# Rwkv6 with a SiLU block: w handled a unit ahead, the state's decay on ScalarE, and another order of the diagonal

## The chip, the core and the metric

The kernel runs on one core of a Trainium2 chip. The core has five engines that run their own instruction streams and wait for each other through semaphores: TensorE (PE in the profile, its weight loads PEld), VectorE (DVE), ScalarE (ACT), GpSimd (POOL) and SyncE (SP), which here only issues transfers. The metric is the device time of one execution in microseconds, smaller is better. The kernel before takes 576.55 us, the median of 3 runs (576.12, 576.55 and 578.34).

## The reference

Two blocks follow each other. The first is a recurrence over 768 tokens, for 4 batches and 8 heads of 48 channels; the second is two matrix products with a SiLU between them, over the 3072 rows that the first one gives.

```python
for t in range(S):                                   # S = 768
    cur = einsum('bhd,bhe->bhde', u * k[t], v[t])
    y[t] = einsum('bhd,bhde->bhe', r[t], state + cur)
    state = w[t][..., None] * state + einsum('bhd,bhe->bhde', k[t], v[t])
x = y.transpose(0, 2, 1, 3).reshape(3072, 384)
h = x @ w_in                                         # 384 x 2048
out = (h * (1 / (1 + exp(-h)))) @ w_out              # 2048 x 384
```

## The kernel before, in words

**Units.** The work is cut into 12 units: 6 chunks of 128 tokens times 2 pairs of batches (`units`, L66). Unit 0 is the first, so the sixth is unit 5. A chunk is not run token by token. With products of w over 2, 4, 8 ... 128 tokens (`product`, L404: levels 0 to 6, each one POOL multiplication that halves the length), queries and keys are scaled level by level (`grow_queries` L621 on VectorE, `grow_keys` L639 and `grow_own` L648 on POOL, `odd_keys` L609 on ScalarE, `prepare` L776 and L778), multiplied on TensorE (`burst`, L697) and kept under a mask in `score` (`keep_level`, L715 on VectorE, L797 on ScalarE). `score` times v, and the state times the queries, give y (`y_state`, L840 and L847; `y_values`, L861). At the end of a chunk the state is multiplied by the product of the whole chunk's w (the decay, L911) and the products of k and v are added (L906 on TensorE, L920 on VectorE): `update`.

**The diagonal.** From unit 4 on the blocks of 8 x 8 tokens on the diagonal of `score` are made apart: `block_bonus` (L490 on POOL, steps 0 to 7) multiplies r, k, u and w elementwise in another layout (`tokens_rk`, `tokens_w`, loaded by `load_rk`, L158); `block_sum` (L527 on VectorE, steps 0 to 4) reduces them into `block_sums`; `block_move` stores these to memory (`kept`, one transfer, L549) and loads them back in the layout of `score` (five transfers, L554 and L556); `block_turn` (L560) and two `block_write` (L566) put them in. Sum 2 needs bonus step 4; sum 3 needs step 6; sum 4 needs step 7.

**Loads and turns.** w, k and r of a unit come in 4 blocks of 32 tokens for each (`load_blocks`, L127, 4 transfers a block, all issued on SP), into one room for each name. `turn` (L361, two VectorE transposes) puts them in the layout of the products; only then may the room be loaded again. v comes by `load_values` (L140 and L147, 5 transfers).

**The second block** is done with fewer multiplications by a Strassen-like scheme. For unit i-1 its first layer is 20 products (`ups`; `first_part`, L1141, 16 matmuls each, 0.87 us of TensorE). They run in the order 20, 18, 14, 13, 2, 15, 4, 7, 19, 16, 1, 12, 9, 11, 3, 6, 10, 5, 8, 17, in four PSUM banks that are reused. Between them are sums and differences of the banks (`join`, L1168 on VectorE), copies (L1162) and SiLUs (L1165, L1184) on ScalarE. So product 4 has to wait for the join behind 13, and product 17 for the join behind 10. The inputs of these products are made by `sums_of_x` (steps 0 to 7, VectorE, L1102 to L1122). The second layer of unit i-2 is 7 quarters (`downs`; `quarter`, L1284, 16 matmuls each, 2.6 us). Their inputs are made by `sums` (8 VectorE instructions, L1255); quarters 0, 2, 3 and 6 end with a copy on ScalarE (L1289), 1, 4 and 5 with a join on VectorE (L1292). Quarters 0, 2, 4 and 6 add into the same bank one after the other, so quarter 6 starts only when the join of quarter 4 has read it.

**The order** is written by hand. `mix(i)` gives 21 groups of steps for unit i, and the last loop puts between the groups the 27 steps `downs(i - 2) + ups(i - 1)`. Every engine gets its instructions in that order and waits in it. TensorE's order around a unit is: 7 quarters, the first `burst` behind quarter 6, products 20 to 11, the second burst, products 3 to 17, then the transposes of k and `y_state`, which end the unit. Group 0 stands ahead of quarters 0 and 1, group 1 ahead of quarter 2, group 2 of 3, group 3 of 4, group 4 of 5 and 6, group 5 of products 20 and 18, group 6 of 14, group 7 of 13, group 8 of 2 and 15, group 9 of 4, groups 10 to 13 of 7, 19, 16 and 1, group 14 of 12 and 9, group 15 of 11, group 16 of 3 and 6, group 17 of 10, group 18 of 5, group 19 of 8 and 17, and group 20 of the next unit's quarter 0.

Of the kernel before, what the change touches and what calls it, by code (L numbers as in the profile page):

```python
# [38 lines left out]
def kernel(  # L39
# [16 lines left out]
    NL = 7  # L56
# [841 lines left out]
    def update(i, b):  # L898
# [50 lines left out]
    def mix(i):  # L949
# [12 lines left out]
        def turns(j):  # L962
            return [*both(turn, j, "w"), (product, j, 0), *both(turn, j, "k")]

        def start(j):
            return [*[(product, j, l) for l in range(1, NL)], (grow_own, j, 1)]
# [16 lines left out]
        else:  # L983
            j = i - 1
            groups = [([*both(turn, i, "r"), (grow_own, i, 0), (x_out, j)], 2),
                      ([*start(i), *bonus_steps(i, 4), (x_in, j), (reverse_v, i)], 1),
                      ([(grow_queries, i, 2), (sums_of_x, j, 0)], 1),
                      ([(odd_keys, i, 2), (grow_keys, i, 2, False), (sums_of_x, j, 1)], 1),
                      ([(sums_of_x, j, 2), *sum_steps(i, 2), (prepare, i, 3), *bonus_steps(i, 5, 6, 7), (sums_of_x, j, 3, 4, 5, 6)], 2),
                      ([(burst, i, 3), (keep_level, i, 3)], 2),  # L990
                      ([*sum_steps(i, 3)], 1),
                      ([], 1),
                      ([*sum_steps(i, 4), (keep_level, i, 4)], 2),
                      ([(go_on, i, 4)], 1),
                      ([], 1),
                      ([*at(ahead, (load_rk, i + 1, (0, 1), nc.scalar)), (block_move, i, False), (block_move, i, True), *at(ahead, (load_rk, i + 1, (2,)))], 1),
                      ([], 1),
                      ([(sums_of_x, j, 7)], 1),
                      ([(prepare, i, 5)], 2),
                      ([], 1),  # L1000
                      ([(burst, i, 5), (keep_level, i, 5, 0), (keep_level, i, 6, 0), (go_on, i, 6), (block_turn, i), (block_write, i, 1)], 2),
                      ([(keep_level, i, 5, 1), (keep_level, i, 6, 1)], 1),
                      ([(block_write, i, 0)], 1),
# [439 lines left out]
```

## Time and profile before

| | |
|---|---|
| median of 3 runs | 576.55 us |
| profiled execution, whole | 580.51 us |
| its span, first to last instruction | 578.6 us |
| granted TensorE clock, mean | 0.997 |
| PE / DVE / POOL / ACT busy | 97% / 82% / 67% / 45% |
| from `y_state` to `y_state`, units 5 to 11 | 45.0, 44.1, 43.6, 43.3, 42.9, 44.6, 42.5 us |
| moved by transfers | 57.59 MB, 206485 packets |

In the rows, the first number of a timeline line is its start in us from the span's start, the second its length, and the brackets hold the idle time of the engine ahead of it and what ended it. A line of the waits has the total in us, how often, and the longest. Rows of the stretches show for each engine the busy time and the number of instructions, then the granted clock, the DMA engines' share and the GB/s. Instructions of an engine can overlap a little at their ends, so a pitch is taken from start to start.

### The profile page before, as it was taken

How to read it: one execution, taken by the hardware profiler on the slowest of the kernel's cores; microseconds unless marked ns; L12 is line 12 of the kernel's file. 1: busy time of each engine (PE TensorE's matmuls, PEld its weight loads, DVE VectorE, ACT ScalarE, POOL GpSimd, SP SyncE). 2: the span in 40 equal slices, each digit the busy share in tenths (PEclk: the TensorE clock that was granted, in tenths of full speed). 3: DMA queues.
4: the chain of work that ended last, by engine and by line, in shares of the span. 5: the costliest groups of instructions: out<-in, count | busy, mean ns of one | idle time of the engine just before them, and what ended most of it. 6: DMA issues, size and time to landing. Idle time of an engine off the chain costs nothing. (4 is left out here: it accounts for less than half of the span.)

```text
span 578.6 us, 18815 instructions
## 1 busy us (share of the span) xinstructions
PE 559.7 (97%) x7782; PEld 519.2 (90%) x7782; DVE 475.8 (82%) x748; ACT 259.1 (45%) x556; POOL 390.4 (67%) x459
## 2 busy tenths in 40 slices
PE   8989999999999899999999999999999989999997
PEld 8767777698899899999989989999999989999997
DVE  7979798898899999889889889889899878782250
ACT  5679695432541370371371372372371362371330
POOL 5998868547799997866866866866976966810000
PEclk9999999999999999999999999999999999999999
DMA  9957776444345453554554454464464452002000
GB/s 224 310 114 207 174 237 101 48 81 114 89 83 76 110 84 70 94 109 86 93 108 92 89 110 85 91 109 89 88 113 89 89 109 60 33 9 56 28 7 22
DMA packets 206485, 57.59 MB, mean 100 GB/s; under 512 B 186048, under 2 KB 198208, under 8 KB 206400
## 3 DMA queue, kind: packets, MB, share of 16 engines
q1 hardware_dynamic: 196272, 44.01, 39.0%
q10 hardware_dynamic: 10128, 12.39, 8.4%
q8 instruction: 61, 1.00, 0.8%
q14 instruction: 24, 0.20, 0.1%
HBM read 47.14 MB, written 9.18 MB: 97 GB/s over the span
## 5 line engine op out<-in xcount | busy, mean ns | idle before, releaser
L639 POOL TENSOR_TENSOR tk<-tk,tw 128x256 f32<-128x256 f32 x128 | 95.3, 765 | 37.0 <-ACT tk L609 27.3
L1284 PE MATMUL p_o<-own,temps 128*128 128x192 f32 x528 | 88.1, 326 | 0.2 <-DVE temps L1255 0.2
L1284 PEld LDWEIGHTS p_o<-own,temps 128*128 128x128 f32 x528 | 86.0, 190 | 0.6 <-DVE temps L1255 0.5
L1141 PE MATMUL p_o<-xt,w_in_sb 128*64 128x128 f32 x1152 | 73.4, 273 | 5.7 <-DVE p_o L1168 5.0
L407 POOL TENSOR_TENSOR tw<-tw 128x256 f32<-128x256 f32 (+6 forms) x83 | 42.4, 510 | 45.1 <-DVE tw L361 41.2
L1141 PEld LDWEIGHTS p_o<-xt,w_in_sb 128*64 128x64 f32 x1152 | 64.6, 137 | 7.1 <-DVE p_o L1168 6.2
L1034 PE MATMUL p_h<-xt,w_in_sb 128*128 128x256 f32 x288 | 66.1, 384 | 1.7 <-POOL w_in_sb L260 1.6
L1034 PEld LDWEIGHTS p_h<-xt,w_in_sb 128*128 128x128 f32 x288 | 53.6, 190 | 10.0 <-POOL w_in_sb L260 2.4
L1284 PE MATMUL p_o<-w_out_sb,gt 128*128 128x192 f32 x340 | 60.0, 329 | 1.6 <-DVE ob L1292 0.9
L490 POOL TENSOR_TENSOR ruk<-tokens_rk 128x384 f32<-128x384 f32 x48 | 54.1, 1148 | 11.1 <-DMA tokens_rk<-in_k_dram 6.8
L1284 PEld LDWEIGHTS p_o<-w_out_sb,gt 128*128 128x128 f32 x340 | 55.3, 190 | 2.8 <-DVE ob L1292 1.2
L1289 ACT COPY partial<-p_o 128x192 f32<-128x192 f32 x33 | 10.5, 319 | 92.3 <-PE p_o L1284 77.5
L621 DVE TENSOR_TENSOR tr<-tr,tw 128x512 f32<-128x512 f32 x61 | 51.3, 841 | 0.5
L609 ACT COPY tk<-tk 128x256 f32<-128x256 f32 x52 | 20.9, 402 | 64.6 <-POOL tk L639 44.6
L1255 DVE TENSOR_TENSOR temps<-gt 128x512 f32<-128x512 f32 (+1 forms) x48 | 43.3, 940 | 0.0
L1165 ACT ACTIVATE gt<-p_o 128x512 f32<-128x512 f32 x45 | 26.0, 601 | 24.7 <-PE p_o L1141 24.7
L715 DVE COPY_PREDICATED score<-mask,p_sc 128x512 f32<-128x512 int8 x42 | 31.2, 799 | 1.8 <-PE p_sc L697 1.6
L1284 PE MATMUL p_o<-w_out_sb,temps 128*128 128x192 f32 x176 | 30.4, 326 | 0.0
L490 POOL TENSOR_TENSOR spare<-tokens_rk 128x384 f32<-128x384 f32 x24 | 29.1, 1227 | 0.6
L1284 PE MATMUL p_h<-w_out_sb,gt 128*128 128x192 f32 x168 | 29.1, 326 | 0.0
L1284 PEld LDWEIGHTS p_o<-w_out_sb,temps 128*128 128x128 f32 x176 | 28.9, 190 | 0.0
L648 POOL TENSOR_TENSOR tk<-tk,tw 128x256 f32<-128x256 f32 x32 | 28.0, 896 | 0.0
(239 smaller groups left out, 1264.2 us busy)
## 6 DMA issues: line engine op xcount, KB each, us to landing
w_out_sb<-in_moe_w_in_dram SPq DMA_DIRECT2D x6, 768.0 KB, 7.3
w_out_sb<-in_moe_w_out_dram SPq DMA_DIRECT2D x4, 768.0 KB, 7.4
own<-in_moe_w_out_dram SPq DMA_DIRECT2D x4, 768.0 KB, 6.6
tokens_w<-in_w_dram SPq DMA_DIRECT2D x8, 384.0 KB, 4.8
turned<-yt ACTq DMA_DIRECT2D x16, 192.0 KB, 2.6
xt<-turned ACTq DMA_DIRECT2D x8, 384.0 KB, 3.7
tokens_rk<-in_r_dram ACTq DMA_DIRECT2D x7, 384.0 KB, 4.4
tokens_rk<-in_k_dram ACTq DMA_DIRECT2D x7, 384.0 KB, 6.2
```

The lines of the kernel that those rows point to most:

```text
L407: engine.tensor_tensor(out=up, in0=t[:, :, 0::2], in1=t[:, :, 1::2], op=ALU.mult)
L490: mul = lambda out, one, two: nc.gpsimd.tensor_tensor(out=out, in0=one, in1=two, op=ALU.mult)
L609: nc.scalar.copy(out=keys(i, X[(l + 1) % 2] * L + c, [4 * c, blocks], [c, 2], [1, c]), in_=keys(i, NP * L + c, [4 * c, blocks], [NP * L + ...
L621: nc.vector.tensor_tensor(out=odd, in0=odd, in1=tw[i][l][:, :, 0::2][:, :, :, None].to_broadcast([128, Q, L >> (l + 1), c]), op=ALU.mult)
L639: nc.gpsimd.tensor_tensor(out=out, in0=have, in1=odd_products(i, l, b, *blocks), op=ALU.mult)
L648: nc.gpsimd.tensor_tensor(out=have, in0=have, in1=odd_products(i, l, b, [2, NP * ni]), op=ALU.mult)
L715: nc.vector.copy_predicated(out=dst, mask=masks[l][:, :, None].to_broadcast([128, NB, NP, ni, c]), data=sc[e].rearrange("p (b q) (i c) -> ...
L1034: nc.tensor.matmul(p_h[:, a, :], lhsT=w_in_sb[:, c, f * 128:(f + 1) * 128], rhs=xt[i][:, c, :], start=(a == 0 and c == 0), stop=(a == 1 an ...
L1141: nc.tensor.matmul(p[h:h + PD, q, :], lhsT=left[:, f:f + PD], rhs=right, start=first and q == 0, stop=q == 3, skip_group_check=True)
L1165: nc.scalar.activation(out=g(f, t), in_=have, func=AF.Silu)
L1255: nc.vector.tensor_tensor(out=out, in0=one, in1=two, op=op)
L1284: nc.tensor.matmul(p, lhsT=left(f), rhs=right[:, f, :], start=which in (0, 1, 3) and f == 0, stop=f == FH - 1, skip_group_check=True)
```

## The change

- **w ahead.** From unit 6 on, w is turned in group 7 of the unit before and its products 0 to 3 and 4 to 6 are made in groups 9 and 16 there; before, they were made at the unit's start. Unit 5 keeps its w at the start, and turns unit 6's w too. The loads of w are issued in groups 13 to 15 of the unit before that (unit 6's: in groups 1 and 2 of unit 5).
- **Loads.** k and the first two blocks of r come in groups 1 to 3, v and the others of r in groups 12 and 13.
- **The decay** of unit 4 and later is done on ScalarE, as eight scaled copies of 48 columns, in group 1 of the next unit, with the state's adds behind them.
- **The diagonal and its neighbours, units 5 and up.** Sum 2 moves from group 4 to group 2, `prepare` of level 3 and bonus step 5 to group 3, `sums_of_x` 0 and 1 to group 3; sums 3 and 4 both go to group 5; `block_move` and the `load_rk` of the next unit go from group 11 to group 6.

```diff
@@ update
-        if n > 0:
+        if n > 0 and i < NPAIR:
             nc.gpsimd.tensor_tensor(out=new, in0=new,
...
-        if b < NB - 1:
+        if b == NB - 1 and i < NPAIR:
+            add_update(i)
+
+    def add_update(i):
+        n, b0 = units[i]
+        if n == S // L - 1:
             return
+        for b in range(NB if i >= NPAIR else 0):
+            for p in range(NP):
+                new = state[:, b0 + b, p, :]
+                nc.scalar.activation(out=new, in_=new, func=AF.Copy, scale=tw[i][NL][:, b * NP + p, :])
         for e in range(2):
...
@@ mix
         def turns(j):
-            return [*both(turn, j, "w"), (product, j, 0), *both(turn, j, "k")]
+            return [*at(j <= NPAIR + 1, *both(turn, j, "w"), (product, j, 0)), *both(turn, j, "k")]
         def start(j):
-            return [*[(product, j, l) for l in range(1, NL)], (grow_own, j, 1)]
+            return [*at(j <= NPAIR + 1, *products_of(j, *range(1, NL))), (grow_own, j, 1)]
+        def products_of(j, *ls):
+            return [(product, j, l) for l in ls]
...
+            else:
+                groups = [([*both(turn, i, "r"), (grow_own, i, 0), (x_out, j)], 2),
+                          ([*at(j >= NPAIR, (add_update, j)), *start(i), *bonus_steps(i, 4), (x_in, j), (reverse_v, i)], 1),
+                          ([(odd_keys, i, 2), (grow_keys, i, 2, False), (grow_queries, i, 2), *sum_steps(i, 2)], 1),
+                          ([(prepare, i, 3), *bonus_steps(i, 5), (sums_of_x, j, 0, 1)], 1),
+                          ([(sums_of_x, j, 2), *bonus_steps(i, 6, 7), (sums_of_x, j, 3, 4, 5, 6)], 2),
+                          ([(burst, i, 3), *sum_steps(i, 3), (keep_level, i, 3), *sum_steps(i, 4)], 2),
+                          ([*at(ahead, (load_rk, i + 1, (0, 1), nc.scalar)), (block_move, i, False), (block_move, i, True), *at(ahead, (load_rk, i + 1, (2,)))], 1),
+                          ([*at(ahead, *both(turn, i + 1, "w"))], 1),
+                          ([(keep_level, i, 4)], 2),
+                          ([(go_on, i, 4), *at(ahead, *products_of(i + 1, 0, 1, 2, 3))], 1),
+                          ([], 1),
+                          ([], 1),
+                          ([], 1),
+                          ([(sums_of_x, j, 7)], 1),
+                          ([(prepare, i, 5)], 2),
+                          ([], 1),
+                          ([(burst, i, 5), (keep_level, i, 5, 0), (keep_level, i, 6, 0), (go_on, i, 6), *at(ahead, *products_of(i + 1, 4, 5, 6)), (block_turn, i), (block_write, i, 1)], 2),
+                          ([(keep_level, i, 5, 1), (keep_level, i, 6, 1)], 1),
+                          ([(block_write, i, 0)], 1),
+                          (end[0], 2), (end[1], 0)]
...
             blocks = block_loads(i + 1, "wkr")
-            for at, some in ((0, blocks[0:3]), (1, blocks[3:6]), (2, [*blocks[6:8]]), (3, [(load_values, i + 1)]),
+            head, tail = (blocks[0:8], blocks[8:]) if i == NPAIR + 1 else (blocks[4:10], blocks[10:])
+            tail += block_loads(i + 2, "w") if i + 2 < len(units) else []
+            for at, some in ((1, head[0:3]), (2, head[3:5]), (3, head[5:]), (12, [(load_values, i + 1), *tail[0:1]]),
+                             (13, tail[1:3]), (14, tail[3:4]), (15, tail[4:])) if i > NPAIR else ((0, blocks[0:3]), (1, blocks[3:6]), (2, [*blocks[6:8]]), (3, [(load_values, i + 1)]),
                              (12, blocks[8:9]), (13, blocks[9:10]), (14, blocks[10:11]), (15, blocks[11:])):
```

More of the change, by code (lines that the diff above doesn't have):

```diff
@@ L984, in mix @@
             j = i - 1
[L985 to L1003, printed above, removed]
-                      (end[0], 2), (end[1], 0)]
@@ new lines, in mix @@
+            if i <= NPAIR:
+                groups = [([*both(turn, i, "r"), (grow_own, i, 0), (x_out, j), *at(j >= NPAIR, (add_update, j))], 2),
+                          ([*start(i), *bonus_steps(i, 4), (x_in, j), (reverse_v, i)], 1),
+                          ([(grow_queries, i, 2), (sums_of_x, j, 0)], 1),
+                          ([(odd_keys, i, 2), (grow_keys, i, 2, False), (sums_of_x, j, 1)], 1),
+                          ([(sums_of_x, j, 2), *sum_steps(i, 2), (prepare, i, 3), *bonus_steps(i, 5, 6, 7), (sums_of_x, j, 3, 4, 5, 6)], 2),
+                          ([(burst, i, 3), (keep_level, i, 3)], 2),
+                          ([*sum_steps(i, 3)], 1),
+                          ([], 1),
+                          ([*sum_steps(i, 4), (keep_level, i, 4)], 2),
+                          ([(go_on, i, 4)], 1),
+                          ([], 1),
[4 more added lines that the diff above has]
+                          ([], 1),
+                          ([(burst, i, 5), (keep_level, i, 5, 0), (keep_level, i, 6, 0), (go_on, i, 6), (block_turn, i), (block_write, i, 1)], 2),
+                          ([(keep_level, i, 5, 1), (keep_level, i, 6, 1)], 1),
[8 more added lines that the diff above has]
+                          ([(burst, i, 3), *sum_steps(i, 3), (keep_level, i, 3), *sum_steps(i, 4)], 2),
+                          ([*at(ahead, (load_rk, i + 1, (0, 1), nc.scalar)), (block_move, i, False), (block_move, i, True), *at(ahead, (load_rk, i + 1, (2,)))], 1),
+                          ([*at(ahead, *both(turn, i + 1, "w"))], 1),
+                          ([(keep_level, i, 4)], 2),
+                          ([(go_on, i, 4), *at(ahead, *products_of(i + 1, 0, 1, 2, 3))], 1),
+                          ([], 1),
+                          ([], 1),
+                          ([], 1),
+                          ([(sums_of_x, j, 7)], 1),
+                          ([(prepare, i, 5)], 2),
+                          ([], 1),
+                          ([(burst, i, 5), (keep_level, i, 5, 0), (keep_level, i, 6, 0), (go_on, i, 6), *at(ahead, *products_of(i + 1, 4, 5, 6)), (block_turn, i), (block_write, i, 1)], 2),
+                          ([(keep_level, i, 5, 1), (keep_level, i, 6, 1)], 1),
+                          ([(block_write, i, 0)], 1),
+                          (end[0], 2), (end[1], 0)]
```

## The prediction

> **What bounds the kernel now.** The page first: TensorE is busy 97% of the span, so only its gaps can be won.
>
> ```profile
> span 578.6 us, 18815 instructions
> PE 559.7 (97%) x7782; PEld 519.2 (90%) x7782; DVE 475.8 (82%) x748; ACT 259.1 (45%) x556; POOL 390.4 (67%) x459
> ```
>
> Then TensorE's waits: most of what is lost in the second half is a wait for a join on VectorE (L1168, L1292), little for anything else.
>
> ```profile
> PE p_o L1141 <- DVE p_o L1168: 6.0, 6, 2.0
> ...
> PE p_o L1284 <- DVE ob L1292: 0.9, 1, 0.9
> ```
>
> By the timeline the L1168 gaps stand before matmul 17, at the end of units 5 to 8 and 10: 0.40, 0.95, 0.99, 0.61 and 2.02 us (none in unit 9). VectorE's own waits in 260 to 475 us say why it is late: it stands for POOL's products of the diagonal and for the diagonal's transfer (spare<-kept), 1.0 to 2.6 us at a time; in unit 9 that transfer came in time.
>
> ```profile
> DVE block_sums L527 <- POOL spare L490: 10.8, 5, 2.2
> DVE spare L560 <- DMA spare<-kept: 6.9, 4, 2.6
> DVE p_o L1168 <- ACT gt L1165: 4.0, 5, 0.8
> DVE block_sums L527 <- POOL ruk L490: 1.9, 5, 0.4
> ```
>
> Unit 9 therefore shows what is left without that stall. VectorE's timeline from the join behind matmul 11 to the join of quarter 4 has no idle time but the first 0.81:
>
> ```profile
> 423.63 0.70 DVE L1168 TENSOR_TENSOR p_o<-p_h,gt 128x512 f32<-128x512 f32 x1 [0.81 <-ACT gt L1165]
> ...
> 424.83 1.26 DVE L621 TENSOR_TENSOR tr<-tr,tw 128x512 f32<-128x512 f32 x1
> ...
> 430.04 2.89 DVE L1255 TENSOR_TENSOR temps<-gt 128x512 f32<-128x512 f32 x2
> ...
> 435.08 1.29 DVE L1255 TENSOR_TENSOR temps<-gt 128x512 f32<-128x512 f32 x2
> ...
> 448.78 0.34 DVE L1292 TENSOR_TENSOR ob<-p_o,partial 128x192 f32<-128x192 f32 x1
> ```
>
> That is 25.5 us (423.63 to 449.12). Quarter 6 adds into the bank that this join reads, and TensorE begins quarter 6 at 449.60: the cover is 0.5 us. In unit 5 it is already gone:
>
> ```profile
> 231.85 2.87 PE L1284 MATMUL p_o<-w_out_sb,gt 128*128 128x192 f32 x16 [0.94 <-DVE ob L1292]
> ```
>
> The two L1255 rows show a second thing: 1.41 us apart while POOL runs its products (until 433.81), 0.61 when it is done. Each POOL instruction between two such VectorE instructions costs VectorE 0.8 us.
>
> Last the clock, by stretches. The window with unit 10's gap (2.02 us idle) is followed by one at half clock; the last whole window (1.55 idle) is not.
>
> ```profile
> 471.33:474.74 3.41, 1.39 (x28) 1.15 (x22) 3.41 (x3) 1.39 (x5) 3.33 (x3) 1.00 0.42 54
> 474.74:478.16 3.42, 3.42 (x64) 2.97 (x62) 3.32 (x5) 2.43 (x5) 1.37 (x1) 0.50 0.42 55
> ...
> 573.73:577.14 3.41, 1.86 (x12) 1.57 (x10) 0.00 (x0) 0.32 (x1) 0.00 (x0) 1.00 0.17 56
> ```
>
> Half clock for 3.41 us loses 1.71. The sum is made against the profiled execution, 580.51 us (span 578.6 and 1.9 around it), 3.96 above the median 576.55. Two of the three timed runs agree within 0.43 and one is 1.8 higher, so I take the median as a run without that half window.
>
> **The change, part by part.**
>
> *Diagonal earlier.* Products, reductions, the store (1 DMA), the loads back (5) and tokens_w (1) go from group 11 to 6 on SP. POOL loses before them product 0 (1.04), products 1 to 6 (3.06) and the decay (0.97 for two), so L490's last pair, now done at 328.7 in unit 7, ends some 5 us sooner and the two waits on L490 go (10.8 + 1.9 in five units). The store then follows join 13's place rather than matmul 4's, some 4 us sooner; from store to last landing it took 8.3 us in unit 9 (417.6 to 425.9) and 10.0 in unit 7 (329.8 to 339.8), so the blocks are there 2.5 to 4 us before L560 asks. SP's later loads queue behind the store's 2 to 3 us round trip but are wanted only in the next unit. So the wait on spare<-kept goes, and with it the gaps before matmul 17: -(0.95+0.99+0.61+2.02) = -4.57, in unit 5 -(0.40+0.23+0.07) = -0.70, the half window -1.71.
>
> *Decay on ScalarE.* Eight copies of 48 columns, 0.20 to 0.26 each (rows L587 and L797), 1.6 to 2.1 us behind quarter 0's copy, where ScalarE idles 4.88 us in unit 7: nothing on the path. Without that cover quarter 2's copy would be late by what exceeds it. The two state adds (1.11) move behind quarter 1's join; VectorE's total is unchanged.
>
> *Loads.* w's 16 DMAs a unit (0.5 us of SP each) move to the end of the unit before, load_values (5) from group 3 to 12, r's first half forward; SP's five waits for w's turn (22.1 us) go. Consumers have 15 us or more: 0. The two tokens loads on ScalarE's queue move to group 6, 1.2 us of issue, behind POOL's last diagonal product; queued behind them is matmul 14's copy, for it join 13, for that matmul 4. I count 0.3 us of cover: 0, bounds 0 and 0.9 a unit (one such issue took 1.46).
>
> *Order on VectorE, units 6 to 10.* Before quarter 4's join w's turn goes (-1.22), and sum step 2 (four reductions, 1.05) and L776 (0.66) come: +0.49, which alone uses the 0.48 of cover. w's turn itself lands in group 7, under the idle time that the L490 waits leave.
>
> *POOL's order.* Product 5 writes the room that L621 of the last level (424.83) still reads, so POOL waits for it; product 6 and the first bonus products then meet the two predicated copies. Bonus steps 0 to 3 (six instructions), begun at 424.54 in unit 9, begin some 3 us later, and all fall among the two-input instructions of VectorE: 6 x 0.8 = 4.8 where unit 9 paid 2.4 among the sums, 0.6 in L621 and some 0.5 elsewhere. So +0.5 to +1.1 on the chain. Its next stretch (grow_queries, sums_of_x) meets grow_own and step 4 rather than short products: -0.1 to +0.5. Together quarter 6 waits about 0.49+0.8+0.3-0.48 = 1.1 us in each of five units: +5.5; bounds 0 and 2.0 a unit. Unit 11 has no state add, and VectorE waits 2.64 there now: 0. By the Trainium skill (SBUF — State Buffer, "SBUF: two separate sides") the loser on the shared port pair blocks for the other's whole instruction: at the 1.0 of an unhindered L490 row the six cost 6.0 and the sum would be some 4 us higher; the 0.8 between rows is what I use.
>
> *Unit 5* has the new order without w ahead: product 0 to 6 still stand before grow_own and step 4.
>
> ```profile
> 221.67 1.04 POOL L407 TENSOR_TENSOR tw<-tw 128x512 f32<-128x512 f32 x1 [3.77 <-DVE tw L361]
> ...
> 225.20 3.06 POOL L407 TENSOR_TENSOR tw<-tw 128x256 f32<-128x256 f32 x6
> 228.22 1.88 POOL L648 TENSOR_TENSOR tk<-tk,tw 128x256 f32<-128x256 f32 x2
> 230.06 2.32 POOL L490 TENSOR_TENSOR ruk<-tokens_rk 128x384 f32<-128x384 f32 x2
> ```
>
> Step 4 ends at 232.38, without the decay about 231.3. VectorE comes to sum step 2 at 229.4 and waits 1.9, then 1.05, 0.66, sums_of_x 2.0 and the join 0.3: 235.2 instead of 231.8, +3.4. (ScalarE's odd-keys copy, now ahead of quarter 3's copy, waits for L648 too and stops quarter 5; that lies inside the same 4.4 us.) TensorE then idles 4.4 us within 7; in about three phases of four a 3.41 us window holds as much as 2.02, so +1.7. By the Trainium skill (TensorE: Matmul & The Clock Gate, Part 1) the gate falls back after an idle window; by that no window here would be wholly idle and the 1.7 go; the stretches above show 1.39 us of work in a window that still cost the clock.
>
> *Sum*: -4.57 -0.70 -1.71 +5.5 +3.4 +1.7 = +3.6 on 580.51. Against the median, which I take without the 1.71: +5.3, 581.9, say 582.
>
> **Rivals.**
>
> 1. The cover holds: quarter 4's join keeps under quarter 6 in units 6 to 10 (0 in place of 5.5), unit 5 pays its 3.4 and perhaps 1.7. 576.55-5.27+3.4 = 574.7, to 576.4. For it: unit 7's join had 1.3 us of cover. Against it: there VectorE had been idle 1.80.
> 2. Faster, past the bound of 0.5% (2.9 us): POOL, freed of the decay, brings step 4 before VectorE asks, so unit 5 pays 1.7 (the two inserted steps) and not 3.4, with 0 later: 576.55-5.27+1.7 = 573.0. It decides if step 4 ends by 229.4; by the rows it is 1.9 late.
> 3. The block sums come early but the blocks do not: six DMAs now share the engines with tokens loads issued at the same time, and L560 still waits. Then -4.57 shrinks towards 0: 586. Against it: 2.5 to 4 us of cover.
> 4. No half window in unit 5, the other terms as forecast: 580.2.
>
> **How the numbers follow.** 0.5% is about what a measurement here can tell. Forecast 0.43, rival 4 0.12, rival 3 0.05, rival 1 0.27, rival 2 0.13. Slower: 0.43+0.12+0.05, less 0.02 for forecasts that stay within the bound, 0.58; same 0.27+0.02, 0.29; faster 0.13. With 2.0 a unit and a second half window the sum is 588; the lower end reaches into rival 2: 573.5 to 588. The forecast's own range is 579 to 588.
>
> **What would show it.** Right: no gap before matmul 17 in units 5 to 10; L527 and L560 wait for nothing in units 6 to 10; one gap of 3 us or more before quarter 6 in unit 5 with sum step 2 waiting on L490, and a half-clock window behind it; gaps of 0.5 to 2 us before quarter 6 in units 6 to 10 on L1292; six L1255 at 1.4 us apart. Wrong: bonus steps that start before L621's last level, quarter 4's join early, or a new wait for raw<-in_w or tokens.

## The result, and the profile after

| | before | after |
|---|---|---|
| median (lowest to highest) | 577.36 us (576.12 to 578.34) | 586.34 us (584.72 to 587.57) |
| ratio, 95% interval | 1 | 1.0155 (1.0120 to 1.0191) |
| profiled execution, span | 580.51, 578.6 us | 585.87, 584.0 us |

The before column has one run more than the three that were known ahead of the prediction. The change costs 9.0 us. The forecast, 582, had the way right and put the loss at 5.3 us; the time lies inside its range (573.5 to 588). Part of what it said of the cause was right, one cause it had set at nothing, and one gain was smaller than the profile made it look.

The page of the kernel after, its first lines. TensorE does the same 7782 matmuls; its share fell because the span grew.

```profile
span 584.0 us, 18864 instructions
PE 561.5 (96%) x7782; PEld 520.7 (89%) x7782; DVE 482.8 (83%) x748; ACT 270.2 (46%) x604; POOL 384.4 (66%) x447
```

TensorE's waits after. The joins of the first layer (L1205, L1168 before) held TensorE for 6.0 us and now hold it for 1.4; the quarters of the second layer (L1321) wait for VectorE's join (L1329) and, which is new, for ScalarE's copy (L1326).

```profile
PE p_o L1321 <- DVE ob L1329: 5.1, 5, 2.6
PE p_o L1321 <- ACT partial L1326: 4.5, 3, 2.3
...
PE p_o L1178 <- DVE p_o L1205: 1.4, 2, 1.0
```

VectorE's waits after, in the same 260 to 475 us that the prediction showed. The waits for POOL's products (L527) and for the diagonal's transfer (L560) were the two longest there; neither is left among the leading lines, which are waits for ScalarE of at most 1.4 us.

```profile
DVE p_h L1205 <- ACT gt L1221: 6.5, 5, 1.4
DVE p_o L1205 <- ACT gt L1202: 4.0, 5, 0.8
DVE p_o L1205 <- ACT gt L1199: 3.5, 5, 1.0
```

By units, from `y_state` to `y_state`, with TensorE's gaps of over 0.1 us in the kernel after. The middle column is a second profiled execution of the kernel before (see below).

| unit | before | before, 2nd | after | gaps in the kernel after |
|---|---|---|---|---|
| 5 | 45.0 | 44.4 | 49.2 | quarter 5 0.95, quarter 6 2.60, product 4 0.45, half clock |
| 6 | 44.1 | 44.3 | 43.1 | quarter 6 0.41 |
| 7 | 43.6 | 43.4 | 44.0 | quarter 2 1.27 |
| 8 | 43.3 | 43.0 | 43.1 | quarter 6 0.40 |
| 9 | 42.9 | 43.0 | 46.6 | quarter 2 2.25, half clock |
| 10 | 44.6 | 42.6 | 42.6 | quarter 6 0.41 |
| 11 | 42.5 | 42.2 | 42.6 | quarter 6 1.24 |
| sum | 306.0 | 302.8 | 311.2 | |

So two units carry the loss: unit 5, which was forecast, and unit 9, which was not. The clock, by the stretches of the kernel after: busy time and instructions of PE, PEld, DVE, ACT and POOL, then the granted clock, DMA share and GB/s. Each time a 3.41 us window in which TensorE worked 0.96 or 1.17 us is followed by one at half clock.

```profile
232.70:236.13 3.43, 0.96 (x6) 0.96 (x7) 3.33 (x7) 0.87 (x2) 3.35 (x5) 1.00 0.37 49
236.13:239.55 3.42, 3.42 (x12) 3.13 (x10) 1.84 (x5) 0.00 (x0) 3.34 (x5) 0.50 0.40 51
399.97:403.39 3.42, 1.17 (x8) 1.13 (x8) 3.39 (x6) 1.50 (x7) 3.42 (x5) 1.00 0.69 121
403.39:406.80 3.41, 3.41 (x12) 3.41 (x11) 3.37 (x8) 0.69 (x4) 1.60 (x2) 0.50 0.61 142
```

### The profile page after: what moved, and what is told of

It reads as the page before. It is cut to its first block, busy times and chain, and to the rows that moved or that the text cites. A ratio compares the mean times of both kernels' runs of the same rounds, so it can differ in the third digit from the quotient of the medians.

```text
span 584.0 us, 18864 instructions
## 1 busy us (share of the span) xinstructions
PE 561.5 (96%) x7782; PEld 520.7 (89%) x7782; DVE 482.8 (83%) x748; ACT 270.2 (46%) x604; POOL 384.4 (66%) x447
## 4 chain that ended last, share of the span: by engine, by line
PE 59%; DVE 13%; SPq 9%; POOL 7%; DMA 5%; issue 4%; ACT 1%; ACTq 1%; DVEq 0%; POOLq 0%
PE p_o L1321 19%; PE p_o L1178 12%; PE p_h L1178 8%; SPq L127 8%; PE p_h L1071 5%; PE p_m L1260 4%; POOL tk L639 2%; PE p_sc L697 2%; PE p_h L1321 2%; DVE temps L1292 2%; DMA raw<-in_w_dram 2%; POOL w_in_sb L260 2%; DVE score L715 2%; DVE block_sums L527 1%; DVE tr L621 1%
## 5 line engine op out<-in xcount | busy, mean ns | idle before, releaser
L639 POOL TENSOR_TENSOR tk<-tk,tw 128x256 f32<-128x256 f32 x128 | 96.1, 771 | 39.3 <-ACT tk L609 27.9
L1321 PE MATMUL p_o<-own,temps 128*128 128x192 f32 x528 | 90.3, 331 | 3.6 <-ACT partial L1326 3.5
L1321 PEld LDWEIGHTS p_o<-own,temps 128*128 128x128 f32 x528 | 87.6, 193 | 4.9 <-ACT partial L1326 4.5
L1178 PE MATMUL p_o<-xt,w_in_sb 128*64 128x128 f32 x1152 | 72.1, 273 | 0.7 <-POOL w_in_sb L1117 0.7
L1321 PE MATMUL p_o<-w_out_sb,gt 128*128 128x192 f32 x340 | 62.1, 337 | 5.8 <-DVE ob L1329 5.1
L1321 PEld LDWEIGHTS p_o<-w_out_sb,gt 128*128 128x128 f32 x340 | 56.6, 194 | 8.1 <-DVE ob L1329 6.5
L621 DVE TENSOR_TENSOR tr<-tr,tw 128x512 f32<-128x512 f32 x61 | 52.6, 863 | 0.7
L1326 ACT COPY partial<-p_o 128x192 f32<-128x192 f32 x33 | 10.5, 318 | 84.2 <-PE p_o L1321 59.3
L1292 DVE TENSOR_TENSOR temps<-gt 128x512 f32<-128x512 f32 (+1 forms) x48 | 44.6, 966 | 0.0
L648 POOL TENSOR_TENSOR tk<-tk,tw 128x256 f32<-128x256 f32 x32 | 25.2, 817 | 22.8 <-DVE tk L361 22.8
L1326 ACT COPY ob<-p_o 128x192 f32<-128x192 f32 x11 | 3.5, 319 | 62.9 <-PE p_o L1321 51.3
L1321 PE MATMUL p_o<-w_out_sb,temps 128*128 128x192 f32 x176 | 30.5, 327 | 0.9 <-ACT partial L1326 0.9
L1321 PEld LDWEIGHTS p_o<-w_out_sb,temps 128*128 128x128 f32 x176 | 28.8, 190 | 1.2 <-ACT partial L1326 1.2
L1205 DVE TENSOR_TENSOR p_h<-p_h,gt 128x512 f32<-128x512 f32 x27 | 18.7, 694 | 12.6 <-ACT gt L1221 12.3
```

The source lines that it names most:

```text
L621: nc.vector.tensor_tensor(out=odd, in0=odd, in1=tw[i][l][:, :, 0::2][:, :, :, None].to_broadcast([128, Q, L >> (l + 1), c]), op=ALU.mult)
L639: nc.gpsimd.tensor_tensor(out=out, in0=have, in1=odd_products(i, l, b, *blocks), op=ALU.mult)
L648: nc.gpsimd.tensor_tensor(out=have, in0=have, in1=odd_products(i, l, b, [2, NP * ni]), op=ALU.mult)
L1178: nc.tensor.matmul(p[h:h + PD, q, :], lhsT=left[:, f:f + PD], rhs=right, start=first and q == 0, stop=q == 3, skip_group_check=True)
L1292: nc.vector.tensor_tensor(out=out, in0=one, in1=two, op=op)
L1321: nc.tensor.matmul(p, lhsT=left(f), rhs=right[:, f, :], start=which in (0, 1, 3) and f == 0, stop=f == FH - 1, skip_group_check=True)
```

## What stops unit 9

ScalarE's timeline at the start of unit 9, first before, then after. At the head of a unit ScalarE copies y (L866), issues the two transfers of y's rows that `x_out` makes (turned<-yt; L930 in the kernel before, L939 in the kernel after), and then copies quarter 0.

```profile
391.60 0.58 ACT L866 COPY yt<-p_m 48x512 f32<-48x512 f32 x1
392.21 0.31 ACTq L930 DMA_DIRECT2D turned<-yt  x1
393.92 0.32 ACT L1289 COPY partial<-p_o 128x192 f32<-128x192 f32 x1 [1.74 <-PE p_o L1284]
```

```profile
393.28 2.36 ACT L866 COPY yt<-p_m 48x512 f32<-48x512 f32 x4 [0.98 <-PE p_m L861]
398.52 3.33 ACTq L939 DMA_DIRECT2D turned<-yt  x2
401.89 0.32 ACT L1326 COPY partial<-p_o 128x192 f32<-128x192 f32 x1 [6.25 <-DMA raw<-in_w_dram]
```

Before, the second transfer was issued 0.03 us after the last copy of y had ended, and quarter 0's copy waited for TensorE alone. After, it was issued 5.90 us after that copy (the two issues fill 398.52 to 401.85, and the second takes 0.31). What released ScalarE was the landing of a load of w, though x has nothing to do with w. The instruction records say how: all transfers of SP and ScalarE take turns on eight completion semaphores (100, 102 to 106, 108 and 110), and each one waits until the transfer that had its semaphore before has landed. Here the second transfer of x took semaphore 110, which a load of w, issued at 398.57, gave back when it landed at 401.46. In the kernel before the same transfer took semaphore 100 from a load of r that had landed at 391.67, before the last copy of y had ended. SP was now issuing w's loads at 0.5 us each, and behind ScalarE's wait stood quarter 0's copy, for which quarter 2 has to wait:

```profile
390.86 9.92 SPq L127 DMA_DIRECT2D raw<-in_w_dram  x16
```

```profile
402.26 1.56 PE L1321 MATMUL p_o<-own,temps 128*128 128x192 f32 x7 [2.25 <-ACT partial L1326]
```

Why this did not happen before is in SP's waits, 260 to 475 us. Before, the first line is 22.1 us in which SP stood for w's turn. After, that wait is gone; SP's longest is now the one for the diagonal's store, and SP runs on with loads into the time of `x_out`.

```profile
SPq L127 <- DVE tw L361: 22.1, 5, 5.3
```

```profile
SPq L554 <- DMA kept<-block_sums: 13.7, 5, 3.9
```

SP's timeline of the kernel before at the same place shows the pause: from the end of the loads of r at 391.24 to the first load of w at 396.04 SP issued nothing, and the two transfers of x went out at 391.02 and 392.21. In the kernel after, the row above has SP issuing w's loads from 390.86 to 400.78.

```profile
383.98 7.26 SPq L127 DMA_DIRECT2D raw<-in_r_dram  x12
396.04 4.26 SPq L127 DMA_DIRECT2D raw<-in_w_dram  x9
```

The lateness of the second transfer of x (its issue less the end of the last copy of y) and the gap before quarter 2 go together in every kernel of this study that has `x_out` in this place and on ScalarE:

| kernel, unit | late by | gap before quarter 2 | difference |
|---|---|---|---|
| before, units 6 to 11, both profiles | 0.03 to 0.51 | none | |
| after 6, 8 and 10 | 2.60, 2.78, 1.25 | none | |
| after 7 and 9 | 4.91, 5.90 | 1.27, 2.25 | 3.64, 3.65 |
| e1_w_loads 7, 8 and 9 | 6.19, 3.84, 4.43 | 2.55, 0.20, 0.79 | 3.64, 3.64, 3.64 |
| e2_unit5 6, 7, 9 and 10 | 3.87, 6.77, 4.20, 4.40 | 0.23, 3.15, 0.61, 0.81 | 3.64, 3.62, 3.59, 3.59 |
| e3_products 7 and 8 | 5.57, 3.64 | 2.06, 0.11 | 3.51, 3.53 |
| e4_decay_pool 6, 7 and 9 | 4.34, 6.28, 6.74 | 0.70, 2.64, 3.10 | 3.64, 3.64, 3.64 |
| e6_unit5_whole 8 and 10 | 7.10, 5.79 | 3.53, 2.15 | 3.57, 3.64 |
| e12_k_first 7 | 4.59 | 1.02 | 3.57 |

In all of them, 3.5 to 3.65 us are hidden, and every microsecond beyond is TensorE's. The Trainium skill (DMA: Bandwidth & Descriptors, "Issuing engines are not separate DMA queues") says that starting transfers from several engines saves only issue time, as all of them share the same DMA engines. No run here measures that sharing. What this case shows is another link between two queues: the second issue on ScalarE came 3.0 us after the first, because it stood for the landing of a transfer of SP's queue.

## The experiments

The times of one set are compared with the kernel before on the same chip, whose median was 577.99 us for the first four, 578.42 for e5 to e8, 578.58 for e9 to e11 and 578.92 for e12; ratios carry the verdicts. In these kernels the line numbers of the second block can lie up to 11 away from those of the kernel after.

### e1_w_loads: w loaded later

```diff
-            head, tail = (blocks[0:8], blocks[8:]) if i == NPAIR + 1 else (blocks[4:10], blocks[10:])
-            tail += block_loads(i + 2, "w") if i + 2 < len(units) else []
+            head, tail = blocks[0:8], blocks[8:]
```

> w is loaded in the unit in which it is turned (groups 1 and 2, as the changed kernel does in unit 5 alone), not two units ahead; all else is the changed kernel. Theory: x_out on ScalarE's queue comes right behind the 16 w loads in program order and waits for the landing of the load eight transfers ahead of it, since the transfers take their semaphores in turn from eight; that held up quarter 0's copy and so quarter 2. Then the gaps before quarter 2 (1.27 and 2.25 us in the profile of after) and the half-clock window behind the second (1.71) go: 3.5 to 5.2 us off 586.3, so 581 to 583. Rival: quarter 2 waits because of the eight decays on ScalarE: no change here, 586.

Measured: 582.83 us (582.20 to 584.86), ratio 1.0088 (1.0054 to 1.0123), 3.5 us less than the kernel after. The time lies where the theory put it, but not for its reason: the stalls did not go. The table above has three of them, 3.54 us in sum, where the kernel after has 3.52. What its profile has less is mainly the half-clock window behind unit 9's gap. SP had nothing to wait for between the loads of r and those of w, so it ran on into the loads of the next unit's first groups, and `x_out` met w there again (its second transfer late by 6.19 us in unit 7).

### e2_unit5: part of unit 5 as before

```diff
+            if i == NPAIR + 1:
+                groups[2:5] = [([(grow_queries, i, 2), (sums_of_x, j, 0)], 1),
+                               ([(odd_keys, i, 2), (grow_keys, i, 2, False), (sums_of_x, j, 1)], 1),
+                               ([(sums_of_x, j, 2), *sum_steps(i, 2), (prepare, i, 3), *bonus_steps(i, 5, 6, 7), (sums_of_x, j, 3, 4, 5, 6)], 2)]
```

> Unit 5 alone gets its former groups 2 to 4 back (sum step 2 and prepare of level 3 behind sums_of_x 0 and 1); all else is the changed kernel. Theory: in unit 5 VectorE waits in sum step 2 for bonus step 4, because products 0 to 6 of w still stand before it on POOL. Then unit 5's gaps of 0.95+2.60+0.45 go back to some 1.2 to 1.6, and its half-clock window goes: 4 to 4.5 us off, 582. Rival: the loss lies in turning two w in unit 5 or in the later groups: less than 1 us off, 586.

Measured: 586.72 us (585.05 to 588.13), ratio 1.0144 (1.0113 to 1.0176): no gain. The gaps before quarters 5 and 6 went as expected (0.91 is left, as in the kernel before), but a gap of 2.83 us came up at product 4, with a half-clock window behind it, so that unit 5 still takes 48.6 us. VectorE's and TensorE's timelines of e2_unit5: sum 3 waits for POOL, and sum 4 and w's turn stand ahead of the join behind 13.

```profile
238.85 0.95 DVE L527 TENSOR_REDUCE block_sums<-spare 128x16 f32<-128x768 f32 x1 [2.83 <-POOL spare L490]
...
241.77 1.29 DVE L361 STREAM_TRANSPOSE tw<-raw 128x512 f32<-128x512 f32 x2
242.99 0.67 DVE L1209 TENSOR_TENSOR p_o<-gt,p_h 128x512 f32<-128x512 f32 x1
```

```profile
243.71 1.24 PE L1182 MATMUL p_o<-gt,in_sum 128*64 128x128 f32 x16 [2.83 <-DVE p_o L1209]
```

The expectation failed, and not the cause: POOL was late as said, and the next VectorE instruction that needs POOL stood ahead of the next join. e6 takes the order back as a whole.

### e3_products: products 4 to 6 not ahead

```diff
-                          ([(go_on, i, 4), *at(ahead, *products_of(i + 1, 0, 1, 2, 3))], 1),
+                          ([(go_on, i, 4), *at(i > NPAIR + 1, *products_of(i, 4, 5, 6)), *at(ahead, *products_of(i + 1, 0, 1, 2, 3))], 1),
...
-                          (..., (go_on, i, 6), *at(ahead, *products_of(i + 1, 4, 5, 6)), (block_turn, i), (block_write, i, 1)], 2),
+                          (..., (go_on, i, 6), (block_turn, i), (block_write, i, 1)], 2),
```

> Products 4 to 6 of w are made in group 9 of their own unit, where POOL idles, in place of group 16 of the unit before; all else is the changed kernel. Theory: they wait for grow_queries of the last level and push the bonus steps among VectorE's sums; without them quarter 4's join comes 0.5 to 1 us earlier, the gaps before quarter 6 (0.41 in units 6, 8 and 10, 1.24 in unit 11) go: 2 to 2.5 us off, 584. Rival: the bonus steps only move, the join stays late by its own two inserted steps: no change, 586.

Measured: 581.01 us (576.73 to 583.84), ratio 1.0034 (1.0003 to 1.0065), 5.3 us less than the kernel after. All gaps before quarter 6 in units 6 to 11 are gone; TensorE's waits in 215 to 500 us are those of unit 5 and of x:

```profile
PE p_o L1321 <- ACT partial L1326: 3.1, 2, 2.1
PE p_o L1321 <- DVE ob L1329: 2.6, 1, 2.6
```

POOL's timelines at the end of unit 9, of the kernel after and of e3_products, show why. In the first POOL stands 1.54 us for VectorE's last use of the old products (the row names L560, which ended last; the wait itself ended at 432.73, 0.04 us after L621 had read them); in the second it goes from the keys straight to the bonus steps, and of the pitches between VectorE's eight sums (L1292) only two are 1.41 us, where the kernel after has four between 1.23 and 1.61.

```profile
432.83 1.42 POOL L407 TENSOR_TENSOR tw<-tw 128x16 f32<-128x16 f32 x2 [1.54 <-DVE spare L560]
434.22 1.96 POOL L490 TENSOR_TENSOR ruk<-tokens_rk 128x384 f32<-128x384 f32 x2
```

```profile
426.73 1.19 POOL L639 TENSOR_TENSOR tk<-tk,tw 128x256 f32<-128x256 f32 x2 [3.58 <-ACT tk L609]
427.88 1.97 POOL L490 TENSOR_TENSOR ruk<-tokens_rk 128x384 f32<-128x384 f32 x2
```

### e4_decay_pool: the decay back on POOL

```diff
-        if n > 0 and i < NPAIR:
+        if n > 0:
             nc.gpsimd.tensor_tensor(out=new, in0=new,
...
-        if b == NB - 1 and i < NPAIR:
+        if b == NB - 1:
             add_update(i)
...
-        for b in range(NB if i >= NPAIR else 0):
-            for p in range(NP):
-                new = state[:, b0 + b, p, :]
-                nc.scalar.activation(out=new, in_=new, func=AF.Copy, scale=tw[i][NL][:, b * NP + p, :])
...
-                          ([*at(j >= NPAIR, (add_update, j)), *start(i), *bonus_steps(i, 4), (x_in, j), (reverse_v, i)], 1),
+                          ([*start(i), *bonus_steps(i, 4), (x_in, j), (reverse_v, i)], 1),
```

> The state's decay and adds are put back as they were (two POOL multiplications and the adds in update); all else is the changed kernel. Theory: the decay on ScalarE costs nothing by itself, POOL gets 1 us more before grow_own: 586 to 588, and the gaps before quarter 2 stay. Rival: the eight ScalarE instructions are what delays quarter 0's or quarter 2's copy: those gaps go, 582.

Measured: 587.11 us (586.14 to 587.95), ratio 1.0149 (1.0116 to 1.0182), the same as the kernel after. The decay on ScalarE costs nothing. The profile shows it from the other side too: with the decay gone from ScalarE, quarter 0's copy still stands, and longer, behind the transfers of x:

```profile
399.60 3.25 ACTq L935 DMA_DIRECT2D turned<-yt  x2
402.89 0.32 ACT L1322 COPY partial<-p_o 128x192 f32<-128x192 f32 x1 [7.09 <-DMA raw<-in_w_dram]
```

### e5_xout: x behind quarter 0's copy

```diff
-                groups = [([*both(turn, i, "r"), (grow_own, i, 0), (x_out, j)], 2),
-                          ([*at(j >= NPAIR, (add_update, j)), *start(i), ...
+                groups = [([*both(turn, i, "r"), (grow_own, i, 0)], 2),
+                          ([(x_out, j), *at(j >= NPAIR, (add_update, j)), *start(i), ...
```

> One edit to the kernel after: x_out moves from the end of group 0 to the start of group 1, so that ScalarE issues x's two transfers behind quarters 0 and 1 and no longer ahead of quarter 0's copy. Theory (the stalls before quarter 2 in units 7 and 9, 1.27 and 2.25 us with a half-clock window behind the second, come from x_out's second transfer, which ScalarE can issue only when a load of w has landed, with quarter 0's copy queued behind it): both stalls go, and with them the half window of 1.71: 1.27 + 2.25 + 1.71 = 5.2 less than the kernel after, 580.7 to 583 us; the gaps before quarter 6 and unit 5's stay as they are. Rival (ScalarE is simply late in those units and the wait moves on): quarter 2's copy, or matmul 1's, waits in place of quarter 0's, a gap stands before quarter 4 instead, and the time stays at 586.

Measured: 586.98 us (584.72 to 590.74), ratio 1.0138 (1.0097 to 1.0178). The rival held, to the letter: no gap before quarter 2 is left, and one stands before quarter 4 in units 5, 7, 8, 9 and 10. (In unit 5 this gap of 2.46 us takes the place of the two before quarters 5 and 6.) ScalarE's timeline in unit 7: the transfers wait for w as in the kernel after, and now the decay, x's way in and the copies of quarters 2 and 3 stand behind them.

```profile
312.17 3.21 ACTq L939 DMA_DIRECT2D turned<-yt  x2
315.43 2.03 ACT L924 ACTIVATE state<-state,tw 128x48 f32<-128x48 f32 x8 [6.78 <-DMA raw<-in_w_dram]
...
318.36 0.32 ACT L1326 COPY partial<-p_o 128x192 f32<-128x192 f32 x1 [0.91 <-DMA raw<-in_k_dram]
```

```profile
318.73 0.43 PE L1321 MATMUL p_o<-own,temps 128*128 128x192 f32 x1 [2.64 <-ACT partial L1326]
```

So the wait is x's; moving the step only chooses who stands behind it. e7_products_xout, which has e3's edit with this one, says the same with a price:

> Two edits to the kernel after: products 4 to 6 are made in group 9 of their own unit and not in group 16 of the unit before (e3_products), and x_out stands at the start of group 1 (e5_xout). Theory (the two causes are independent of one another): e3_products' 581.0 less the 2.06 us that it still lost before quarter 2 of unit 7 and less the half window behind that, 1.7: 577.3 us, within 0.5% of the kernel before; what is left is unit 5's 3.6 us and its half window. Rival (the two share a cause, as ScalarE's late quarter 0 copy also makes quarter 6's join late): not better than 581.

Measured: 584.49 us (581.85 to 585.57), ratio 1.0081 (1.0052 to 1.0110). By the ratios that is 0.5% slower than e3_products alone, with gaps of 0.91 to 2.60 us in each of units 5 to 10. The theory of two independent gains fell, since this edit gains nothing.

### e6_unit5_whole and e8_three

```diff
+            if i == NPAIR + 1:
+                groups[2:12] = [...
+                                ([(burst, i, 3), (keep_level, i, 3)], 2),
+                                ([*both(turn, i + 1, "w"), *sum_steps(i, 3)], 1),
+                                ([], 1),
+                                ([*sum_steps(i, 4), (keep_level, i, 4)], 2),
+                                ([(go_on, i, 4), *products_of(i + 1, 0, 1, 2, 3)], 1),
+                                ([], 1),
+                                ([(load_rk, i + 1, (0, 1), nc.scalar), (block_move, i, False), (block_move, i, True), ...], 1)]
```

> One edit to the kernel after: unit 5 gets groups 2 to 11 in the order of before as a whole (sum step 2 and bonus steps 5 to 7 in group 4, the diagonal's store in group 11), with w(6) turned in group 6 ahead of sum step 3 and products 0 to 3 of unit 6 in group 9, so that unit 6 still finds its w done. Theory (unit 5 lost its 0.95 + 2.60 us and its half window because its VectorE work was put ahead of POOL's bonus steps; with e2 only the wait moved on, to the join behind matmul 13): unit 5 shows no gap over 1.2 us and no half window, about 4.5 us less than the kernel after, 582 us. Rival (w of unit 6 turned a unit ahead costs unit 5 the same wherever it stands): a gap of 2 to 3 us stays in unit 5 before one of matmuls 4 to 17, and the time is within 1 us of 586.

Measured: 582.99 us (581.95 to 586.43), ratio 1.0081 (1.0047 to 1.0115), 3.4 us less than the kernel after. Unit 5 takes 45.4 us in place of 49.2, with gaps of 0.93 before quarter 6 and 1.25 at product 17 (the theory allowed 1.2) and no half-clock window there. The profiled execution, 586.43 us, was the longest of the seven: it has gaps of 3.53 and 2.15 before quarter 2 in units 8 and 10, each with a half-clock window. It is the order of unit 5's VectorE work that cost it, and not w of unit 6. e8_three puts e3, e5 and e6 together:

> Three edits to the kernel after: those of e7_products_xout, and unit 5 with its groups 2 to 11 in the order of before (e6_unit5_whole). Theory (three causes, each a place in the order: products 4 to 6 ahead of the turn of the year's join, x_out ahead of quarter 0's copy, unit 5's sums ahead of the bonus steps): nothing over 1.2 us of idle TensorE is left from unit 5 on, no half window, 577.3 - 4.5 = 573 us, faster than before by 0.8%. Rival (VectorE is the next bound and takes most of it back): 576 to 578, no different from before.

Measured: 583.31 us (581.11 to 585.48), ratio 1.0079 (1.0053 to 1.0104). Neither the expected sum nor the rival's: it has e5's edit in it, and of TensorE's waits from 215 to 500 us this one line is nearly all, in units 5, 8 and 10.

```profile
PE p_o L1332 <- ACT partial L1337: 7.5, 3, 3.2
```

### e9_x_sync and e10_three_sync: x on SP

```diff
-                groups = [(..., (x_out, j)], 2),
-                          (..., (x_in, j), (reverse_v, i)], 1),
+                groups = [(..., (x_out, j, nc.sync)], 2),
+                          (..., (x_in, j, nc.sync), (reverse_v, i)], 1),
```

> One edit to the kernel after: from unit 5 on, x_out's two transfers and x_in's one are issued by SP and no longer by ScalarE, at the same places in the order. e5_xout has shown that x_out held behind it whatever ScalarE had next (quarter 0's copy in the kernel after, quarter 1's and 2's in e5_xout). Theory (ScalarE stands because its transfers wait for w's loads to land): with no transfer of x on ScalarE's queue no gap before quarter 2 or 4 is left that waits for ScalarE's copy (4.5 us in all in the kernel after, 0.95 of it the odd-keys copy of unit 5, which stays, and 1.71 for the half-clock window behind the longest): 5.2 less than the kernel after, 581 us; x has 13 us until its first matmul, so SP's wait for it costs nothing. Rival (the copies are late for another reason, or the loads that now stand behind x on SP come late): no faster than 585, with gaps at matmuls that wait for raw or tokens.

Measured: 600.11 us (598.88 to 600.75), ratio 1.0366 (1.0336 to 1.0396). Half of the theory held: no quarter from unit 6 on waits for ScalarE's copy. But on SP the transfers of x stood behind the loads of w in its order, and the second transfer of x was issued 7.0 to 10.6 us behind the last copy of y in units 6 to 10 (1.25 to 5.90 in the kernel after). I had counted 13 us until x's first matmul and had overlooked VectorE: the first step of `sums_of_x` (L1139) stands ahead of quarter 4's join. VectorE's and TensorE's timelines of e9_x_sync, unit 6:

```profile
279.94 0.74 DVE L1139 TENSOR_TENSOR xt<-xt 128x256 f32<-128x256 f32 x1 [3.78 <-DMA xt<-turned]
280.72 1.10 DVE L1142 TENSOR_TENSOR gt<-xt 128x256 f32<-128x256 f32 x1
281.85 0.36 DVE L1329 TENSOR_TENSOR ob<-p_o,partial 128x192 f32<-128x192 f32 x1
```

```profile
282.26 1.01 PE L1321 MATMUL p_o<-w_out_sb,gt 128*128 128x192 f32 x2 [4.59 <-DVE ob L1329]
```

> The three causes taken away together: products 4 to 6 in group 9 of their own unit (e3_products), unit 5's groups 2 to 11 in the order of before (e6_unit5_whole), and x's transfers on SP (e9_x_sync). e8_three, the same but for x's transfers behind quarter 1 on ScalarE, ran at 583.3 and showed three gaps before quarters 2 or 4 of 2.50, 3.18 and 1.78 us, all with quarters' copies late on ScalarE behind x's transfer, and one half-clock window. Theory: these go, 583.3 - 7.5 - 1.7 = 574 us; what is left against the kernel before is then the gain that the prediction gave to the earlier diagonal, 5.3 less (its own gaps before matmul 17). Rival (the loads' waits return on another engine): 578 or more, not faster than before.

Measured: 598.44 us (592.34 to 601.62), ratio 1.0292 (1.0245 to 1.0339): the same wait, and neither of the other two edits can show beside it.

### e11_before_again: the kernel before, profiled again

> The kernel before, unchanged, profiled a second time, since its profiled execution of 580.5 us lies above the median of its timed ones, 576.6. Theory (the half-clock window behind unit 10's gap comes only in some executions, as it hangs on when the diagonal's transfer lands): the gaps before matmul 17 are there again with other sizes, none or one of them with a half window behind, and the time is 576 to 578.5 without one. Rival: the same gaps and window as in the first profile, 580 to 581.

Measured: 577.35 us, span 575.5. The gaps before product 17 are 1.09 in unit 6, 0.59 in unit 7, 0.13 in unit 10 and none in units 5, 8 and 9, 1.81 us in sum; in the first profile they were 4.97, with a half-clock window. TensorE's waits in 215 to 500 us, and VectorE's wait for the diagonal's transfer in 260 to 475 us, which was 6.9 us in the first profile:

```profile
PE p_o L1141 <- DVE p_o L1168: 1.7, 2, 1.1
```

```profile
DVE spare L560 <- DMA spare<-kept: 4.1, 3, 1.9
```

The theory held: what the diagonal's transfer costs changes from one execution to the next, and the execution that the prediction was made from was a dear one (580.51 us, above all four timed ones).

### e12_k_first: give SP its wait back

```diff
-                          ([*at(ahead, *both(turn, i + 1, "w"))], 1),
+                          ([], 1),
                           ([(keep_level, i, 4)], 2),
-                          ([(go_on, i, 4), *at(i > NPAIR + 1, ...
+                          ([(go_on, i, 4), *at(ahead, *both(turn, i + 1, "w")), *at(i > NPAIR + 1, ...
...
-            head, tail = (blocks[0:8], blocks[8:]) if i == NPAIR + 1 else (blocks[4:10], blocks[10:])
-            tail += block_loads(i + 2, "w") if i + 2 < len(units) else []
+            head, tail = (blocks[0:8] if i == NPAIR + 1 else [*blocks[4:8], *blocks[0:4]]), blocks[8:]
```

The lines are shown against the kernel after with the edits of e3 and e6, which this kernel has too; `x_out` is in the place that it has in the kernel after.

> e8_three with x_out back at the end of group 0 on ScalarE, and the loads in another order: unit i loads k of unit i+1 first (groups 1 and 2; SP must wait there for k's turn of unit i, some 6 us behind the new state) and w of unit i+1 behind it (group 3), w's turn moves from group 7 to group 9, and nothing is loaded two units ahead. Theory (in the kernel before, SP's wait for w's turn kept SP's queue empty just when ScalarE issues x_out, so that x_out found its semaphores free and its second transfer followed the first by 1.2 us; the change took that wait away): SP waits again, now for k's turn, x_out's second transfer follows by 1.2 to 1.5 us in every unit from 6 on, no gap is left before quarter 2 or 4, and the time is 583.3 - 7.5 - 1.7 = 574 us. Rival (loads that start later come too late for w's turn, for which VectorE then stands ahead of matmul 11's join, or the gaps were not x_out's): 578 or more.

Measured: 576.42 us (574.40 to 577.83) against 578.92 us, ratio 0.9954 (0.9929 to 0.9980): 0.5% less than the kernel before, with an interval just clear of 1, and some 10 us less than the kernel after. TensorE's waits in 215 to 500 us, ScalarE's timeline in unit 9, and SP's wait for k's turn in 260 to 475 us:

```profile
PE p_o L1188 <- DVE p_o L1215: 1.9, 3, 1.4
PE p_o L1331 <- DVE ob L1339: 1.3, 2, 0.8
PE p_o L1331 <- ACT partial L1336: 1.2, 2, 1.0
```

```profile
392.19 2.20 ACTq L939 DMA_DIRECT2D turned<-yt  x2
394.44 0.32 ACT L1336 COPY partial<-p_o 128x192 f32<-128x192 f32 x1 [3.16 <-DMA turned<-yt]
```

```profile
SPq L127 <- DVE tk L361: 5.6, 4, 2.0
```

The second transfer of x follows the first by 1.48 to 2.00 us in units 6 to 10, where 1.2 to 1.5 was expected, but the first comes late too. So the second is late by 1.40, 2.69, 2.80 and 2.32 us in units 6, 8, 9 and 10, inside the 3.5 that are hidden; in unit 7 it is late by 4.59, and there one gap of 1.02 is left. No window from unit 5 on is at half clock. The time is 2.4 us above the expected 574. Three orders differ from e8_three at once here (x's place, the loads, w's turn), and none was tried alone. That SP's wait did it is not shown: SP's wait for k's turn is 5.6 us, where the wait for w's turn was 22.1 before and the kernel after already had 4.3 for k's turn. What the records do show is that the transfers which hold `x_out` here are loads of r and no longer loads of w.

## Why the prediction was right or wrong

**Diagonal earlier: right in kind, too large.** No gap stands before product 17 in units 5 to 10, and L527 and L560 wait for nothing that counts there. But the 4.57 + 0.70 + 1.71 us were the price in one execution. I took the half window off the median and left the gaps in it; the second profile, at 577.35 us, has 1.81 before product 17 (0.13 in unit 10, not 2.02). So the gain was set 3.2 us too high: 2.8 for units 6 to 10, and 0.4 for unit 5.

**Loads at 0: wrong, and the cause that was missed.** I counted SP's 22.1 us of waiting as time that the change frees and asked only whether the loads come in time. While SP waited, no new load took a semaphore that `x_out` needed; that this wait alone kept `x_out` clear is argued from the traces, not tried by itself. A gap of 1.27 us followed in unit 7, and one of 2.25 with a half window in unit 9, which took 3.7 us more than before: 4.9 us where the sum has 0. That `x_out` holds ScalarE, and what that costs, is shown by e5 and the table of the lateness. The prediction named a new wait for raw<-in_w among the things that would make it wrong, and that is what came, but it had given it no price.

**Decay at 0: right** (e4_decay_pool).

**POOL's order and quarter 6 in units 6 to 10: the mechanism right, the size too large.** Product 5 waits for the last level (1.54 us at the end of unit 9, 1.55 at the end of unit 10), the bonus steps start late, and the first sums run at about 1.4 us. VectorE's timeline of the kernel after, from the join behind 11 into unit 10:

```profile
430.80 0.70 DVE L1205 TENSOR_TENSOR p_o<-p_h,gt 128x512 f32<-128x512 f32 x1 [0.81 <-ACT gt L1202]
...
437.25 2.90 DVE L1292 TENSOR_TENSOR temps<-gt 128x512 f32<-128x512 f32 x2
440.07 1.50 DVE L1292 TENSOR_TENSOR temps<-temps,gt 128x512 f32<-128x512 f32 x1
...
457.04 0.36 DVE L1329 TENSOR_TENSOR ob<-p_o,partial 128x192 f32<-128x192 f32 x1
```

From the join behind 11 to the end of quarter 4's join it is 26.6 us (430.80 to 457.40), against 25.5 before. The added 1.1 is near the 0.49 + 0.8 of the sum (whose 0.5 to 1.1 for POOL was itself set a little low: its parts, 4.8 less 2.4, 0.6 and 0.5, leave 1.3); four pitches between the sums are above 1.2 us, where six at 1.4 were forecast; the 0.3 for the tokens loads on ScalarE did not show, and quarter 6 waited 0.41 in units 6, 8 and 10. In units 7 and 9 it waited for nothing, since quarter 2's stall had just held TensorE longer. That is 1.2 us in place of 5.5 in this execution. e3_products gained 5.3 in the medians when it took these gaps and unit 11's away, and its profile shows 2.5 of it as gaps. Of the 4.9 between the spans of the two profiled executions, another 1.35 are smaller gaps before quarter 2, 0.45 is the gap at product 4 and 0.5 lies ahead of unit 5. Whether those come from the edit stays open, as only one execution of each is profiled.

**Unit 11 at 0: wrong.** Quarter 6 waited 1.24 us. VectorE had indeed waited 2.64 there, but over the whole stretch 5.3 us of its 26.5 were waiting (2.62 of it for the diagonal); the new stretch is 26.1 us long without either wait.

**Unit 5: right in cause and nearly in size.** Quarter 5 waited 0.95 for the odd-keys copy and quarter 6 waited 2.60 behind sum step 2, which waited 1.85 for POOL; the half-clock window came. With 0.45 at product 4 that is 4.00 of gaps, less the 0.94 that was there before: 3.1 where 3.4 was forecast. The sign that the prediction named, one gap of 3 us or more before quarter 6, did not come as such: the loss stood in two places. TensorE's and VectorE's rows of the kernel after:

```profile
229.70 2.87 PE L1321 MATMUL p_o<-w_out_sb,temps 128*128 128x192 f32 x16 [0.95 <-ACT partial L1326]
235.17 4.55 PE L1321 MATMUL p_o<-w_out_sb,gt 128*128 128x192 f32 x16 [2.60 <-DVE ob L1329]
```

```profile
231.39 1.13 DVE L527 TENSOR_REDUCE block_sums<-ruk 128x4 f32<-128x192 f32 x4 [1.85 <-POOL ruk L490]
```

**The sum.** With the terms as measured against the second profile of before: -1.81 (product 17), +4.9 (x), +2.5 (quarter 6, with unit 11), +2.6 and +0.45 (unit 5), +1.7 (its window), and -0.55 for two short waits of TensorE for POOL (0.23 and 0.32) that the second profile has and the kernel after has not: +9.8, where the two spans differ by 8.5 and the medians by 9.0. Most of the 1.3 too much is in waits too short for the table: in the second profile of before, the first matmul of product 4 starts 0.34 to 0.35 us behind the one ahead of it in units 6 and 8 to 11, in the kernel after 0.10 to 0.20, which makes 1.1 us. Two errors of opposite sign, 4.3 too much for quarter 6 in units 6 to 10 and 3.2 too much gain before product 17, nearly cancel with unit 11's 1.2; what is left is the term that was set at nothing. That the time fell inside the range is so in part luck: unit 5 was foreseen, the stall of `x_out` was not, and the room that the range had for it was meant for longer gaps before quarter 6 and a second half window.

## What to carry to other kernels

A wait that looks like waste on an issuing queue can be what keeps that queue clear for another: before a load is freed to run ahead, ask which transfers are issued in the time that it moves into, on any queue, and what stands behind them on their engine. Moving a step that waits does not remove the wait; it changes who stands behind it, and the next engine's in-order list (here VectorE's L1139) decides the price. A gap that hangs on a transfer should be priced from two profiled executions, not from one.

## What the runs showed of the hardware that was not expected

Transfers issued by ScalarE were held by transfers issued by SP: with eight completion semaphores in turn and loads of w at 0.5 us each, the second transfer of x was issued 2.6 to 5.9 us late in units 6 to 9, and TensorE lost whatever was over 3.6 us of that.

A window does not have to be idle to cost the clock: windows with 0.96, 1.17 and (before) 1.39 us of matmuls out of 3.41 were followed by half clock, one with 1.86 was not. The Trainium skill (TensorE: Matmul & The Clock Gate, "What's actually happening") gives the fallback after at least one idle window; these windows were idle for 59% to 72%, so here the measurement decides. All 14 profiles together draw the line more sharply. Taken from 195 us on, in the 3.41 us windows in which the clock steps, all 21 windows with 2.00 us or more without a matmul were followed by half clock, and none of the 1562 with 1.96 us or less; of the two at 1.99 us, one was and one was not.

So where a gap falls matters as much as its length: e5's gap of 2.64 us in unit 7 was cut by a window's edge into 1.07 and 1.57 us and left no half window, while e3's of 2.06 in the same unit lay with 2.01 us in one window and did. Measured by the starts of the same matmuls in the second profile of before, a half-clock window cost 1.7 and 1.8 us in the kernel after (units 5 and 9), and 1.3 in the first profile of before, where small matmuls stood in it.
